# Two ways of cutting the first expert's 448 rows in a fused attention and mixture-of-experts kernel

## The chip, the cores and the metric

The kernel runs on one core of a Trainium2 chip. The metric is the device time of one execution in microseconds (us). The core has a matrix engine (TensorE, PE in the rows; its weight loads are PEld), a vector engine (VectorE, DVE), a scalar engine (ScalarE, ACT), a general engine (GpSimd, POOL) and a queue that issues DMAs (SyncE, SP). Each of them works through its own instructions in the order in which they stand, and waits for the others by semaphores.

## The reference, cut to what matters

Attention over 2 batches of 768 tokens is followed by a mixture of 8 experts, in which each of the 1536 tokens goes to two experts, and by a dense layer pair. `attn_out` below is the attention's output as rows of 512 numbers.

```python
logits = x @ w_gate                                   # x: (1536, 512), the attention's output
noisy_logits = logits + np.log1p(np.exp(x @ w_noise)) * noise
top2 = np.argpartition(-noisy_logits, 2, axis=1)[:, :2]
...
for e in range(8):
    for k in range(2):
        mask = top2[:, k] == e
        h = np.maximum(x[mask] @ w1[e], 0.0)          # 512 -> 1024
        out[mask] += top2_w[mask, k, None] * (h @ w2[e])   # 1024 -> 512
...
h = x @ w_in                                          # the dense pair, 512 -> 2048 -> 512
return (h - np.tanh(h)) @ w_out
```

With the inputs of `setup_inputs()` the experts 0 to 7 get 358, 364, 398, 396, 398, 396, 379 and 383 tokens; of expert 0's, 182 are of batch 0 and 176 of batch 1.

## The kernel before

**Precision.** Every matrix product is made of three products in the type fp32r: a high part of the weights by a high part of the rows, the same weights by the low part of the rows, and the low part of the weights by the high part of the rows. So a tile `hh` holds the high part `hh` and the low part `hl` of a hidden layer, and `xh`, `xl` are the parts of an expert's input rows.

**Segments.** An expert has room for 448 rows (`CAP`). Expert 0 is cut in two segments, the others are one segment each; `segs` (L109) lists them as expert, part, first row, rows, and the number of 128-row blocks next to a shorter tail. Segment 0 is the first 192 rows of expert 0 (`FIRST`), all of which come from batch 0; segment 1 is its other 256 rows. Either has two blocks, of 96 and of 128 rows.

**The products of a segment.** The hidden layer has 1024 units, in eight steps f of 128. In a step the first layer makes 12 products (4 pieces of the depth by 3), whose columns are the segment's rows; `h_out` then lets ScalarE write `hh` (L1306) and VectorE `hl` (L1308). The second layer takes three products of 512 columns for each block (`y_mm`, L1315 to L1317); only the third of them reads `hl`. A short tail of rows is not a block: its high and low parts stand side by side as one stationary operand (`tail_arm`, L1282). The first layer of segments 1 and later chooses among several widths at run time (`ARMS`, `pick_arm`), by the number of rows that an expert got; the number is written by VectorE into `arm` and loaded by TensorE.

**Work in the gaps.** Segment 0 can be computed while batch 1's gate is still being worked out: the gate is a chain of small steps that goes back and forth between VectorE and TensorE. `seg_fine` yields after each piece of segment 0 (half a first layer of a step, or one block's second layer), and `fill` hands pieces out between the steps of the gate: `FILL` and `FILL2` are the numbers of pieces, `left` counts what remains, and `KEEP` pieces are held back for after the gate. `TX` says at which values of `left` segment 1's input rows are transposed (`trans_x`). From the attention to the end of the gate the order on TensorE, VectorE, ScalarE and SyncE is the order in which the code issues; GpSimd's, and the stretch after the gate, follow a scheduler until the order is written by hand again.

**The gate of batch 1.** Its steps, in order: `gate_mm` (L639), the logits and the two best experts on VectorE (L642 to L760, ending in the table `M`), the running counts on TensorE (L776), `where` (L779), six one-hot tables `hot` for the rows that segment 1 takes (`mark`, L819), their products on TensorE (`find`, L828), the indices `xidx` (L829) and two gathers by GpSimd (L835); then the totals (L924, L928), the number of rows for `arm` (L930 to L918), the excess over `CAP` (`exs`, `cmi`), and the target rows `sidx` (L854). With `sidx` GpSimd scatters the tokens to the experts' places in the tensor `Xg`: 12 indirect DMAs of 128 rows each (L858).

**After the gate.** Segment 1's eight steps run. During them SyncE stores segment 0's result (L1343) and loads segment 2's input from `Xg` (L1215, L1218), which needs the scatters; VectorE writes the table `yidx` (L854, a second use of the helper); and TensorE transposes segment 2's rows in steps 5 and 6 of segment 1 (L1228). Then come segments 2 to 8 and the dense pair.

Of the kernel before, what the change touches and what calls it, by code (L numbers as in the profile page):

```python
# [9 lines left out]
F16 = mybir.dt.float16  # L10
# [15 lines left out]
TX = (4, 4, 2, 2)  # L26
# [10 lines left out]
CAP = 448  # L37
# [19 lines left out]
KEEP = 8  # L57
# [4 lines left out]
FIRST = 192  # L62
# [5 lines left out]
ARMS = {0: ((104, 0), (128, 0)),  # L68
# [20 lines left out]
def body(tc, q, k, v, proj, w_gate, w_noise, noise, w1, w2, w_in, w_out, out):  # L89
# [19 lines left out]
    segs = [(0, 0, 0, FIRST, 2), (0, 1, FIRST, CAP - FIRST, 2)]  # L109
# [5 lines left out]
    with ExitStack() as ctx:  # L115
# [489 lines left out]
        idx0 = gx.tile([128, 2], F16, name="idx0")  # L605
        xidx = gx.tile([128, 2], I32, name="xidx")
# [214 lines left out]
        def find(b):  # L821

            ps = bank("a")
            cols = lambda t: [t.rearrange("p (q j) -> p j q", j=2)[:, j] for j in range(2)]
            mms = [(j, id16, idx0[:, j:j + 1]) for j in range(2 * b)]
            mms += [(j, l_, ids[:, b * NC + c:b * NC + c + 1]) for c in range(NC) for j, l_ in enumerate(cols(hot(b, c)))]
            for n, (j, l_, r_) in enumerate(mms):
                nc.tensor.matmul(ps[:, j:j + 1], l_, r_, start=(n == 0), stop=(n >= len(mms) - 2), skip_group_check=True)  # L828
            nc.vector.tensor_copy(xidx if b else idx0, ps[:, 0:2])  # L829

        def gather_x():

            t = hd["xy"][:, 2:4]
            for j in range(2):
                nc.gpsimd.indirect_dma_start(out=t[:, j], out_offset=None, in_=Xd,  # L835
                                             in_offset=bass.IndirectOffsetOnAxis(ap=xidx[:, j:j + 1], axis=0))
            xgs[1] = (t, None)
# [382 lines left out]
        def trans_x(n, dc):  # L1220
# [6 lines left out]
            for j, m_ in enumerate([m] * nb + [128] * (tail > 0)):  # L1227
                nc.tensor.transpose(ps[:, j * m:j * m + m_], xgs[n][0][:m_, j, ck(dc)], ident[:m_, :m_])  # L1228
# [90 lines left out]
        def y_banks(n):  # L1319
            return [bank(t) for t in ("cc" if n == 0 else "dd" if n < B else "ccdd")]  # L1320
# [41 lines left out]
        def seg_fine(n):  # L1362
# [5 lines left out]
            for f in range(NF + 1):  # L1368
                if f < NF:
# [45 lines left out]
        left = [4 * NF]  # L1415
# [388 lines left out]
```

## Time and profile before

| | us |
|---|---|
| runs of the kernel before | 874.85, 876.32, 876.75; median 876.32 |
| the profiled execution | 875.33 |
| its span, first to last instruction | 873.4 |
| TensorE busy | 858.3 (98% of the span) |
| VectorE busy | 665.9 (76%) |
| ScalarE busy | 537.5 (62%) |
| GpSimd busy | 399.7 (46%) |

The span leaves out 1.9 us that lie around it. TensorE is busy nearly all the time, in all of the 40 slices of the page; but that share is no statement on any one stretch. The stretches that the change touches are the gate of batch 1 (272 to 297 us of the span) and segment 1 (301 to 329 us). There the order of the waits is what counts.

### The profile page before, as it was taken

What the parts mean: (1) busy time and instruction counts of PE and PEld (TensorE: products, weight loads), DVE (VectorE), ACT (ScalarE), POOL (GpSimd) and SP (SyncE); (2) the same over time, 40 slices, a digit from 0 to 9 for tenths busy, and PEclk for the clock granted to TensorE, in tenths of its full rate; (3) what the DMA queues carried; (4) which work ended last, traced back from release to release, by engine and by line L of the source; (5) the groups of instructions that cost most, each with busy time, mean ns of one, the idle gap of its engine ahead of it and who ended that gap; (6) DMA issues with size and microseconds to landing.
All of it is one profiled execution on the core that took longest, in us unless ns stands there. A gap on an engine that the chain in (4) does not pass through costs nothing.

```text
span 873.4 us, 13678 instructions
## 1 busy us (share of the span) xinstructions
PE 858.3 (98%) x4621; PEld 673.4 (77%) x4621; DVE 665.9 (76%) x1275; ACT 537.5 (62%) x1028; POOL 399.7 (46%) x390
## 2 busy tenths in 40 slices
PE   8999999999999999999999999999999999999998
PEld 3556555555556889798988889898899999999996
DVE  7688778778775654989798979967886676677665
ACT  7667668667455244545444544567787677677665
POOL 6687787798776644210000008521432622632322
PEclk9999999999999999999999999999999999999999
DMA  5646645411133688797977978563300200200001
GB/s 129 151 116 201 211 127 175 153 43 37 53 112 104 217 288 270 237 323 240 306 259 255 309 262 298 193 238 120 94 22 1 88 22 1 85 25 0 25 13 37
DMA packets 111980, 127.52 MB, mean 146 GB/s; under 512 B 33744, under 2 KB 82944, under 8 KB 111888
## 3 DMA queue, kind: packets, MB, share of 16 engines
q1 hardware_dynamic: 105680, 110.52, 40.0%
q0 software_dynamic: 5008, 15.49, 5.2%
q8 instruction: 57, 0.93, 0.4%
q10 hardware_dynamic: 1200, 0.30, 0.2%
q14 instruction: 35, 0.29, 0.1%
HBM read 82.81 MB, written 41.18 MB: 142 GB/s over the span
## 4 chain that ended last, share of the span: by engine, by line
PE 57%; DVE 4%; ACT 2%; issue 1%; DMA 1%; POOL 0%; SPq 0%; DVEq 0%; ACTq 0%; POOLq 0%
PE bank L1275 13%; PE bank L1317 9%; PE bank L1315 9%; PE bank L1316 9%; PE bank L1237 4%; PE bank L1235 4%; PE bank L1236 4%; PE bank L1282 2%; PE bank L1228 1%; DVE wt L1010 1%; DMA xy<-Xg 1%; DVE g_u L1604 1%; PE bank L1573 1%; DMA wraw<-in_moe_w_dram 0%; DVE hh L1622 0%
## 5 line engine op out<-in xcount | busy, mean ns | idle before, releaser
L1315 PE MATMUL bank<-wt,hh 128*128 128x512 f32 (+1 forms) x392 | 155.5, 397 | 2.2 <-PEq L1253 1.2
L1317 PE MATMUL bank<-wt,hh 128*128 128x512 f32 (+1 forms) x392 | 155.2, 396 | 1.3 <-DVE hh L1308 1.2
L1316 PE MATMUL bank<-wt,hh 128*128 128x512 f32 (+1 forms) x392 | 153.9, 393 | 0.0
L1597 POOL TENSOR_TENSOR g_th<-g_h,g_th 128x384 f32<-128x384 f32 x64 | 66.9, 1046 | 183.3 <-ACT g_th L1596 182.6
L1275 PE MATMUL bank<-xh,wt 128*128 128x400 f32 (+3 forms) x512 | 139.0, 335 | 0.0
L481 ACT ACTIVATE p<-bank 128x384 f32<-128x384 f32 x192 | 91.8, 488 | 67.5 <-PE bank L480 56.7
L446 DVE TENSOR_REDUCE mx<-bank 128x1 f32<-128x384 f32 x192 | 103.3, 551 | 36.6 <-PE bank L445 34.5
L1010 POOL TENSOR_TENSOR wt<-wraw,wt 128x512 fp32r<-128x512 f32 x30 | 48.7, 1642 | 143.5 <-DVE xy L1347 137.1
L1275 PEld LDWEIGHTS bank<-xh,wt 128*128 128x128 f32 x512 | 92.7, 188 | 1.8 <-issue 0.3
L1011 ACT ACTIVATE wt<-wraw 128x1024 fp32r<-128x1024 f32 x75 | 78.9, 1055 | 19.4 <-PE bank L1317 17.0
L1317 PEld LDWEIGHTS bank<-wt,hh 128*128 128x128 f32 (+1 forms) x392 | 73.1, 186 | 20.5 <-DVE hh L1308 2.1
L1237 PE MATMUL bank<-xh,wt 128*128 128x384 f32 x256 | 86.4, 337 | 0.0
L1315 PEld LDWEIGHTS bank<-wt,hh 128*128 128x128 f32 (+1 forms) x392 | 73.2, 187 | 17.0 <-issue 2.4
L1235 PE MATMUL bank<-xh,wt 128*128 128x384 f32 x256 | 86.2, 337 | 0.0
L1236 PE MATMUL bank<-xl,wt 128*128 128x384 f32 x256 | 86.0, 336 | 0.0
L1275 PE MATMUL bank<-xl,wt 128*128 128x400 f32 (+3 forms) x256 | 84.7, 331 | 0.9 <-DVE xl L1230 0.9
L514 POOL TENSOR_TENSOR ps<-ps,p 128x768 f32<-128x768 f32 x45 | 82.3, 1829 | 7.3 <-ACT p L481 3.1
L1306 ACT ACTIVATE hh<-bank 128x448 fp32r<-128x448 f32 (+2 forms) x72 | 36.1, 502 | 79.5 <-issue 22.7
L1316 PEld LDWEIGHTS bank<-wt,hh 128*128 128x128 f32 (+1 forms) x392 | 73.2, 187 | 13.2
L505 PE MATMUL bank<-p,v 128*64 128x384 f32 x384 | 83.1, 512 | 0.0
L479 PE MATMUL bank<-qc,kb 108*128 108x384 f32 (+1 forms) x192 | 78.9, 411 | 1.1 <-DVE qc L469 1.0
L1010 DVE TENSOR_TENSOR wt<-wraw,wt 128x1024 fp32r<-128x1024 f32 (+1 forms) x64 | 73.9, 1158 | 3.9 <-ACT wt L1011 3.6
(319 smaller groups left out, 1819.7 us busy)
## 6 DMA issues: line engine op xcount, KB each, us to landing
wraw<-in_moe_w_dram SPq DMA_DIRECT2D x118, 256.0 KB
cv_t<-in_moe_w_in_dram SPq DMA_DIRECT2D x16, 512.0 KB
cv_t<-in_moe_w_out_dram SPq DMA_DIRECT2D x16, 512.0 KB
W2f<-cv_w SPq DMA_DIRECT2D x16, 512.0 KB
wraw<-W2f SPq DMA_DIRECT2D x16, 512.0 KB
Xg<-zero SPq DMA_DIRECT2D x14, 512.0 KB
xy<-Xg SPq DMA_DIRECT2D x7, 768.0 KB
Y<-xy SPq DMA_DIRECT2D x7, 768.0 KB
```

The source lines that it names most:

```text
L446: nc.vector.tensor_reduce(MX[i % 2][:, c, hf:hf + 1], ps[:, :HF], op=ALU.max, axis=AX.X)
L481: nc.scalar.activation(hd["p", i, kc][:, half(hf)], ps[:, :HF], AF.Exp, scale=float(D) ** -0.5)
L505: nc.tensor.matmul(hd["o", i][hf * D:(hf + 1) * D, :HF], raw["v", g][:, par, kc], hd["p", i, kc][:, half(hf)], start=(kc == 0), stop=(kc = ...
L514: eng.tensor_tensor(t, hd["p", i, 0] if kc == 1 else t, hd["p", i, kc], op=ALU.add)
L1010: low = lambda eng, h: eng.tensor_tensor(t[:, 1, h], r[:, h], t[:, 0, h].bitcast(F32), op=ALU.subtract)
L1235: nc.tensor.matmul(ps[:, :n], ws(0, dc), xh[:, dc, :n], start=(dc == 0), stop=False)
L1236: nc.tensor.matmul(ps[:, :n], ws(0, dc), xl[:, dc, :n], start=False, stop=False)
L1237: nc.tensor.matmul(ps[:, :n], ws(1, dc), xh[:, dc, :n], start=False, stop=(dc == KD4 - 1))
L1275: nc.tensor.matmul(col(ps), t[:, w_, 0, ck(dc)], col(x_[l_][:, dc]), start=(dc == 0 and (w_, l_) == (0, 0)), stop=(dc == KD4 - 1 and w_ == 1))
L1315: nc.tensor.matmul(ps[:m], a, t[:, 0, 1], start=first, stop=False)
L1316: nc.tensor.matmul(ps[:m], a, t[:, 1, 1], start=False, stop=False)
L1317: nc.tensor.matmul(ps[:m], l, t[:, 0, 1], start=False, stop=last)
```

## The change

Expert 0 is cut at row 128 instead of 192. Segment 0 becomes one block of 128 rows; segment 1 becomes 320 rows, in two blocks of 128 and a tail of up to 64. That is three blocks for expert 0 instead of four.

- Segment 0's first layer hands its 128 columns to each product twice (`twice`), so a product has 256 columns.
- Segment 1 gets four widths instead of two. A row count of at most 360 takes the first: two times 116 columns, no tail. Choosing takes two more VectorE instructions (L917) for `arm`.
- `find` and `gather_x` handle 320 rows: the one-hot tables have 320 columns instead of 256, there are three products for each token chunk instead of two (18 and 21 instead of 12 and 14), one more copy after each (L829), and three gathers instead of two. `trans_x` of segment 1 makes three transposes for each piece instead of two, and that of segment 0 one instead of two.
- There are 24 pieces of segment 0 instead of 32. `FILL` and `FILL2` stay; `KEEP` and `TX` become 4 and (1, 1, 0, 0).
- The accumulators in PSUM: segment 0 takes one bank, segment 1 three (`y_banks`).

```diff
-TX = (4, 4, 2, 2)
+TX = (1, 1, 0, 0)
...
-KEEP = 8
+KEEP = 4
...
-FIRST = 192
+FIRST = 128
...
-ARMS = {0: ((104, 0), (128, 0)),
+ARMS = {0: ((116, 0), (128, 0), (128, 16), (128, 64)),
...
-    segs = [(0, 0, 0, FIRST, 2), (0, 1, FIRST, CAP - FIRST, 2)]
+    segs = [(0, 0, 0, FIRST, 1), (0, 1, FIRST, CAP - FIRST, 2)]
...
-            cols = lambda t: [t.rearrange("p (q j) -> p j q", j=2)[:, j] for j in range(2)]
-            mms = [(j, id16, idx0[:, j:j + 1]) for j in range(2 * b)]
+            cols = lambda t: [t[:, 0:256].rearrange("p (q j) -> p j q", j=2)[:, j] for j in range(2)] + [t[:, 256:NL]]
+            some = lambda j: slice(0, 128 if j < 2 else NL - 256)
+            mms = [(j, id16[some(j), some(j)], idx0[some(j), j:j + 1]) for j in range(3 * b)]
...
-            nc.vector.tensor_copy(xidx if b else idx0, ps[:, 0:2])
+            o_ = xidx if b else idx0
+            nc.vector.tensor_copy(o_[:, 0:2], ps[:, 0:2])
+            nc.vector.tensor_copy(o_[some(2), 2:3], ps[some(2), 2:3])
...
-            t = hd["xy"][:, 2:4]
-            for j in range(2):
-                nc.gpsimd.indirect_dma_start(out=t[:, j], out_offset=None, in_=Xd,
-                                             in_offset=bass.IndirectOffsetOnAxis(ap=xidx[:, j:j + 1], axis=0))
+            t = hd["xy"][:, 1:4]
+            for j in range(3):
+                r = slice(0, 128 if j < 2 else NL - 256)
+                nc.gpsimd.indirect_dma_start(out=t[r, j], out_offset=None, in_=Xd,
+                                             in_offset=bass.IndirectOffsetOnAxis(ap=xidx[r, j:j + 1], axis=0))
...
-            return [bank(t) for t in ("cc" if n == 0 else "dd" if n < B else "ccdd")]
+            return [bank(t) for t in ("c" if n == 0 else "cdd" if n < B else "ccdd")]
...
+                    twice = lambda a_: a_[:, None, :rows].to_broadcast([128, 2, rows])
...
-                            nc.tensor.matmul(ps[:, :rows], ws(t, w_, dc), x_[:, dc, :rows], start=st_, stop=sp_)
+                            nc.tensor.matmul(ps[:, :2 * rows].rearrange("p (t n) -> p t n", t=2), ws(t, w_, dc), twice(x_[:, dc]),
+                                             start=st_, stop=sp_)
...
-        left = [4 * NF]
+        left = [3 * NF]
```

The order on two engines moves with it, since a step of segment 0 is three pieces instead of four while `FILL` stays. In the rows below a buffer's number tells tiles apart; the weights of steps 2, 3, 4 and 6 are wt_1522, wt_1908, wt_2286 and, in the changed kernel, wt_3432.

TensorE, before, at the running counts of the gate (L776): the second layer of step 2 stands ahead of them, and step 3's first layer ahead of that.

```order
L1376 MATMUL bank2_3275<-xh_3296,wt_1908 128x192
L1315 MATMUL bank4_3497<-wt_1143,hh_3493 96x512
...
L1315 MATMUL bank5_3496<-wt_1522,hh_3591 96x512
L1316 MATMUL bank5_3496<-wt_1522,hh_3591 96x512
L1317 MATMUL bank5_3496<-wt_1522,hh_3591 96x512
L1315 MATMUL bank4_3497<-wt_1522,hh_3591 96x512
L1316 MATMUL bank4_3497<-wt_1522,hh_3591 96x512
L1317 MATMUL bank4_3497<-wt_1522,hh_3591 96x512
L776 LDWEIGHTS before_182
L776 MATMUL bank1_3662<-M_198,before_182 128x48
```

The same place now.

```order
L1321 MATMUL bank5_3492<-wt_1522,hh_3583 128x512
L1381 MATMUL bank3_3277<-xh_3296,wt_2286 128x256
...
L1319 MATMUL bank5_3492<-wt_1908,hh_3649 128x512
L1320 MATMUL bank5_3492<-wt_1908,hh_3649 128x512
L1321 MATMUL bank5_3492<-wt_1908,hh_3649 128x512
L776 LDWEIGHTS before_182
L776 MATMUL bank1_3673<-M_198,before_182 128x48
```

Step 4's first layer and step 3's second layer have moved ahead of the running counts.

VectorE, before, from the totals to the excess.

```order
L928 COPY tots<-bank_3724 128x24
L930 TENSOR_TENSOR cnt<-tots 1x8
L931 TENSOR_TENSOR cnt<-cnt,basev 1x1
L915 TENSOR_SCALAR acc<-cnt 1x1
L918 CAST arm<-acc 1x1
L935 TENSOR_TENSOR exs<-tots 128x8
L936 TENSOR_TENSOR exs<-exs,capv 128x8
L937 TENSOR_SCALAR exs<-exs 128x8
L1308 SCALAR_TENSOR_TENSOR hh<-bank_3275,hh 128x192
L940 TENSOR_REDUCE cmx<-exs 128x1
```

The same place now.

```order
L932 COPY tots<-bank_3747 128x24
L1312 SCALAR_TENSOR_TENSOR hh<-bank_3277,hh 128x128
L934 TENSOR_TENSOR cnt<-tots 1x8
L935 TENSOR_TENSOR cnt<-cnt,basev 1x1
L919 TENSOR_SCALAR acc<-cnt 1x1
L921 SCALAR_TENSOR_TENSOR acc<-cnt,acc 1x1 x2
L922 CAST arm<-acc 1x1
L939 TENSOR_TENSOR exs<-tots 128x8
L940 TENSOR_TENSOR exs<-exs,capv 128x8
L941 TENSOR_SCALAR exs<-exs 128x8
L944 TENSOR_REDUCE cmx<-exs 128x1
```

The low part of a step of segment 0 stood between L937 and L940, that of step 5; now a low part, that of step 6, stands right behind the totals, and ahead of everything that is worked out from them.

TensorE, now, around that step's first layer and the totals (L928, L931).

```order
L1321 MATMUL bank5_3492<-wt_2286,hh_3667 128x512
L1381 MATMUL bank3_3277<-xh_3296,wt_3432 128x256
...
L928 LDWEIGHTS onesb_180
L928 MATMUL bank1_3747<-M_198,onesb_180 128x8
...
L931 MATMUL bank1_3747<-M_198,onesb_180 128x8
L1381 MATMUL bank3_3277<-xh_3296,wt_3432 128x256
```

Step 6's first layer is cut in two by the totals; before, two second layers of step 3 stood ahead of the totals and the first layer of step 5 behind them.

## Rows read from the trace of the kernel before

**Rows 1.** Stretches: us; busy PE, PEld, DVE, ACT, POOL; granted clock; DMA share, GB/s.
```profile
272.00:297.00 25.00, 24.66 (x216) 20.48 (x214) 18.03 (x84) 7.12 (x15) 14.48 (x14) 1.00 0.37 124
297.00:320.00 23.00, 21.79 (x142) 18.69 (x141) 13.45 (x41) 10.11 (x19) 13.94 (x13) 1.00 0.85 298
```

**Rows 2.** TensorE in order of time, segment 1: start, us, instructions, [idle before <-releaser].
```profile
316.20 0.50 PE L1317 MATMUL bank<-wt,hh 128*128 128x512 f32 x1 [0.91 <-DVE hh L1308]
...
320.14 0.49 PE L1228 MATMUL bank<-ident,xy 128*128 128x128 f32 x3
320.82 0.76 PE L1228 MATMUL bank<-ident,xy 128*128 128x128 f32 x5 [0.18 <-DMA xy<-Xg]
```

**Rows 3.** VectorE in order of time, segment 1.
```profile
314.15 0.17 DVE L854 CAST yidx<-g_p 128x12 int32<-128x12 f32 x1 [2.43 <-DMA Xg<-x,sidx]
...
314.60 1.22 DVE L1010 TENSOR_TENSOR wt<-wraw,wt 128x1024 fp32r<-128x1024 f32 x1
315.73 0.42 DVE L1308 SCALAR_TENSOR_TENSOR hh<-bank,hh 128x256 fp32r<-128x256 f32 x1
```

**Rows 4.** SyncE's queue in order of time: the store of segment 0, the load of segment 2.
```profile
314.04 0.33 SPq L1343 DMA_DIRECT2D Y<-xl  x1
...
314.92 0.69 SPq L1218 DMA_DIRECT2D xy<-Xg  x1
```

**Rows 5.** GpSimd in order of time: a gather, the first scatter after the gate, the last.
```profile
290.23 0.96 POOL L835 DMA_INDIRECT xy<-Xd,xidx  x1 [0.30 <-issue]
294.54 1.78 POOL L858 DMA_INDIRECT Xg<-x,sidx  x1 [3.35 <-DVE sidx L854]
...
309.42 0.98 POOL L858 DMA_INDIRECT Xg<-x,sidx  x1 [0.31 <-issue]
```

**Rows 6.** VectorE in order of time, the gate of batch 1.
```profile
285.86 0.35 DVE L1308 SCALAR_TENSOR_TENSOR hh<-bank,hh 128x192 fp32r<-128x192 f32 x1
286.64 0.22 DVE L779 SCALAR_TENSOR_TENSOR where<-bank,late,M 128x6 f32<-128x6 f32 x1 [0.43 <-PE bank L776]
286.90 1.29 DVE L819 TENSOR_SCALAR xT<-zero,where 128x256 f16<-128x256 f16 x6
...
290.33 0.18 DVE L928 COPY tots<-bank 128x24 f32<-128x24 f32 x1 [1.19 <-PE bank L927]
290.55 0.16 DVE L930 TENSOR_TENSOR cnt<-tots 1x8 f32<-1x8 f32 x1
...
292.12 0.36 DVE L1308 SCALAR_TENSOR_TENSOR hh<-bank,hh 128x192 fp32r<-128x192 f32 x1 [0.40 <-ACT hh L1306]
292.39 0.15 DVE L940 TENSOR_REDUCE cmx<-exs 128x1 f32<-128x8 f32 x1
...
294.09 0.17 DVE L854 CAST sidx<-g_p 128x12 int32<-128x12 f32 x1
294.19 2.36 DVE L1010 TENSOR_TENSOR wt<-wraw,wt 128x1024 fp32r<-128x1024 f32 x2
```

**Rows 7.** TensorE in order of time, gate of batch 1, then the start of segment 1.
```profile
286.13 0.20 PE L776 MATMUL bank<-M,before 128*128 128x48 bf16 x1
...
288.31 0.45 PE L1315 MATMUL bank<-wt,hh 128*96 128x512 f32 x1
...
289.76 0.45 PE L924 MATMUL bank<-M,onesb 128*128 128x8 bf16 x12
...
290.15 0.34 PE L1376 MATMUL bank<-xh,wt 128*128 128x192 f32 x1
...
291.56 0.39 PE L1315 MATMUL bank<-wt,hh 128*96 128x512 f32 x1
...
301.09 0.26 PE L1275 MATMUL bank<-xh,wt 128*128 128x208 f32 x1
```

**Rows 8.** The chain that ended last: start, us, what; twelve products of 208, then of 372 columns.
```profile
305.32 1.32 PE bank L1275 x12
...
325.18 2.05 PE bank L1275 x12
```

More of the change, by code (lines that the diff above doesn't have):

```diff
@@ L604, in body @@
         ids = zero[:, NL // 2 + 64:NL // 2 + 64 + B * NC // 2].bitcast(F16)
-        idx0 = gx.tile([128, 2], F16, name="idx0")
-        xidx = gx.tile([128, 2], I32, name="xidx")
+        idx0 = gx.tile([128, 3], F16, name="idx0")
+        xidx = gx.tile([128, 3], I32, name="xidx")
         where = gx.tile([128, B, NC], F32, name="where")
@@ L823, in find @@
             ps = bank("a")
-            cols = lambda t: [t.rearrange("p (q j) -> p j q", j=2)[:, j] for j in range(2)]
-            mms = [(j, id16, idx0[:, j:j + 1]) for j in range(2 * b)]
+            cols = lambda t: [t[:, 0:256].rearrange("p (q j) -> p j q", j=2)[:, j] for j in range(2)] + [t[:, 256:NL]]
+            some = lambda j: slice(0, 128 if j < 2 else NL - 256)
+            mms = [(j, id16[some(j), some(j)], idx0[some(j), j:j + 1]) for j in range(3 * b)]
             mms += [(j, l_, ids[:, b * NC + c:b * NC + c + 1]) for c in range(NC) for j, l_ in enumerate(cols(hot(b, c)))]
             for n, (j, l_, r_) in enumerate(mms):
-                nc.tensor.matmul(ps[:, j:j + 1], l_, r_, start=(n == 0), stop=(n >= len(mms) - 2), skip_group_check=True)
-            nc.vector.tensor_copy(xidx if b else idx0, ps[:, 0:2])
+                nc.tensor.matmul(ps[some(j), j:j + 1], l_, r_, start=(n == 0), stop=(n >= len(mms) - 3), skip_group_check=True)
+            o_ = xidx if b else idx0
+            nc.vector.tensor_copy(o_[:, 0:2], ps[:, 0:2])
+            nc.vector.tensor_copy(o_[some(2), 2:3], ps[some(2), 2:3])
         def gather_x():
-            t = hd["xy"][:, 2:4]
-            for j in range(2):
-                nc.gpsimd.indirect_dma_start(out=t[:, j], out_offset=None, in_=Xd,
-                                             in_offset=bass.IndirectOffsetOnAxis(ap=xidx[:, j:j + 1], axis=0))
+            t = hd["xy"][:, 1:4]
[3 more added lines that the diff above has]
+                                             in_offset=bass.IndirectOffsetOnAxis(ap=xidx[r, j:j + 1], axis=0))
             xgs[1] = (t, None)
@@ L1226, in trans_x @@
             ps = bank("a")
-            for j, m_ in enumerate([m] * nb + [128] * (tail > 0)):
+            for j, m_ in enumerate([m] * nb + [tail if n < B else 128] * (tail > 0)):
                 nc.tensor.transpose(ps[:, j * m:j * m + m_], xgs[n][0][:m_, j, ck(dc)], ident[:m_, :m_])
```

## The prediction

> **What bounds the kernel now.** I read first the stretches [rows 1]: in the gate of batch 1 TensorE works 24.66 of 25 us, so a product taken out there looks like time won. Then I read who ends TensorE's waits behind that stretch, in order of time. In segment 1 TensorE waits twice: 0.91 us at 316.20 for the low part of a step, and 0.18 us at 320.82, in the middle of the transposes of segment 2's rows, for the load of these rows [rows 2]. Both waits hang on one thing that TensorE has no part in. On VectorE the low part (315.73) stands behind a weight split (314.60), and that behind the table `yidx`, for which VectorE sat idle 2.43 us until the last scatter had landed, at 314.15 [rows 3]. On SyncE's queue segment 0's store went out at 314.04, at the same landing, and the load of segment 2's rows behind it, its last part at 314.92 [rows 4]; in the rows it lands just before 320.82. So a second chain runs beside TensorE's products: gate, `sidx`, 12 scatters, landing, low part and load, transposes. TensorE arrives 0.9 us early at the one place and 0.2 us early at the other. The time is set by that chain as far as the transposes, and by TensorE's products behind them. Products saved ahead of 316 us lengthen the wait there; they shorten nothing unless the scatters land earlier too. The question is what the change does to `sidx`.
>
> **What it takes from TensorE.** The second layer of expert 0 loses 24 products of 512 columns. Six of them took 1.45 us (288.31 to 289.76) [rows 7], 0.24 each with their start: 5.6 us. Segment 0's 96 first-layer products grow from 192 to 256 columns. The trace has no such product of 256; twelve of 192 took 1.41 us (290.15 to 291.56) [rows 7], twelve of 208 took 1.32 and twelve of 372 took 2.05 us [rows 8]. So 192 and 208 cost alike, about 0.11 each, and 372 costs 0.171. For 256 I take 0.118, near the narrow rows since it is nearer to them; the ends are 0.11 and, on a line from 208 to 372, 0.128. That adds 0.8 us (0 to 1.7). Segment 1's 96 products go from 208 to 232 columns: 0.3 us by the same reckoning (0 to 0.9). Thirteen more of the tiny products of `find`, at 0.45 us for twelve [rows 7], add at most 0.5 us; the tail's one product 0.24. The transposes go from eight to four for segment 0 and from eight to twelve for segment 1: nil. TensorE is left with some 3.8 us less to do before the transposes of segment 2.
>
> By the Trainium skill ("TensorE: Matmul & The Clock Gate", section "Back-to-back issue gap") an isolated product takes its columns at 2.4 GHz and 2.5 ns, which makes 82 ns for 192 columns and 109 for 256, and would price the doubled columns at 2.6 us instead of 0.8. The rows disagree at 192 columns (0.11), so I keep theirs.
>
> **What it does to `sidx`, step by step.** The trace shows all the pieces; only their order is new.
>
> (1) The running counts (L776) began at 286.13 [rows 7]. Step 3's second layer now stands ahead of them, and its third product needs the low part of step 3, which VectorE writes only behind the table `M`: 285.86, 0.35 long [rows 6]. It is ready near 286.2, the product takes 0.23, the counts begin near 286.5: **+0.4 us** (0.3 to 0.5), and `where` (286.64) with them.
>
> (2) The six one-hot tables behind `where` took 1.29 us at 256 columns [rows 6]. At 320 they cost at least nothing more and at most a quarter more, 0.32; I take **+0.2**, because small instructions of VectorE in the same rows last 0.15 whatever they hold. The last products of `find` wait for the last table, so TensorE goes on at about 288.9 instead of 288.31.
>
> (3) From there to the totals TensorE had six second-layer products, 1.45 us [rows 7]. Now it has three (0.7) and half a first layer (0.7): the same.
>
> (4) The totals come 0.6 later, VectorE's copy (290.33) [rows 6] near 290.9. Directly behind it VectorE now has the low part of step 6, whose second half of the first layer TensorE begins behind the totals: 0.7 us, and the lag to the low part, 0.56 (291.56, end of step 5's products, to 292.12) [rows 6, 7]. VectorE waits until about 292.0, and `cnt` begins near 292.2 instead of 290.55 [rows 6]: **+1.65**. What is queued behind that wait is everything that leads to `sidx`.
>
> (5) From `cnt` to `sidx` the rows have 3.54 us (290.55 to 294.09) [rows 6]. The low part of step 5, which stood in between, cost 0.40 of waiting and 0.27 of its own: about **-0.65**. Two more small instructions for `arm`, at about 0.2 each (290.33 to 290.55) [rows 6]: **+0.4**. So `sidx` comes near 295.5: **+1.4 us** in all. Without growth of the tables it is +1.2, with a quarter and slow products +1.75.
>
> **From `sidx` to the end.** GpSimd sat idle 3.35 us ahead of the first scatter [rows 5]. The second gather began at 290.23 and takes 1.26 with its gap [rows 5]; 0.6 later and with a third behind it, GpSimd is free near 293.4, and the third is covered; were `sidx` two microseconds earlier it would not be. The twelve scatters go out between 294.54 and 309.42 [rows 5], one behind the other, whatever TensorE does, so they land 1.4 later, near 315.5. VectorE's low part follows at the distance that it had (314.15 to 315.73 [rows 3]), and TensorE's third product of that step at 317.6 instead of 316.20. TensorE waits for it for some 3.4 us: it came at 315.3 before (316.20 less 0.91) and comes near 314.2. (Not 3.8 earlier, since it is held up already on the way: behind `sidx` VectorE has two weight splits, 2.36 us [rows 6], so until 298.0; then the low part of step 7, 0.3, which the last product of segment 0 waits for; then come six transposes, some 0.7 (five took 0.76 to their last end [rows 2]). Segment 1 begins near 299.2 instead of 301.09 [rows 7], and spends about 0.8 more: on the low parts of rows just transposed, for which no product is left as cover, on the tail's product and on wider columns.) From the third product to the transposes lie 3.94 us (316.20 to 320.14) [rows 2]: 321.5, and the point where TensorE waited for the load comes at 322.0. The load lands 1.4 later, less what segment 0's store no longer carries: 128 KB at about 0.3 MB/us [rows 1], 0.4 us; so near 321.8, no wait there. TensorE goes on at 322.0 instead of 320.82: **+1.2 us**. Behind it the work is as before, but for segment 1's tail bank, whose two evacuations segment 2's tail waits for: 0.1. The sum is **+1.3 us**.
>
> The profiled execution took 875.33, the median of three is 876.32, their mean 875.97. 875.33 + 1.3 is 876.6; against the median it is 877.6. I predict 877.1, between the two.
>
> **The rivals.**
>
> *The saving gets through.* If VectorE's wait for the landing is an ordering that falls away, or the low part of step 6 is no obstacle because TensorE reaches it sooner, `sidx` stays where it was or comes earlier, and part of the 3.8 us arrives: 871.5 if all, 873.5 if half. For it speaks TensorE's share of 24.66 in 25 us [rows 1]; against it that the idle 2.43 us on VectorE and the store at 314.04 end at one landing [rows 3, 4], and that in the new order of VectorE the wait is written down. Chance 0.16.
>
> *The clock falls.* The granted clock is 1.00 in both stretches [rows 1], that is 2.4 GHz, and the longest wait in them is 0.91 us [rows 2]. A wait of 3.4 us is new. If TensorE's clock dropped to 1.2 GHz behind it, each microsecond of products would take two: up to 3.9 us more by the transposes, so 879 to 881. It decides from the point where the wait at 316.20 is long enough. No row at the lower level stands against or for it. Chance 0.12.
>
> The Trainium skill ("TensorE: Matmul & The Clock Gate", Part 1) says that an idle TensorE falls back to the lower level and has to earn the higher one again; no row here shows a fall.
>
> *A wider arm.* Expert 0 has 358 rows by the reference and 360 is the first arm's limit. If the kernel counted over 360, tail products would come back, two a step at 0.24: 3.4 us, of which the wait of 3.4 us swallows those ahead of 316 and 1.4 remain: 878.5. Chance 0.02.
>
> **How the numbers follow.** The forecast, a chain that comes 1.3 us later (0.9 to 2.0), has 0.70; with the spread of the runs shown (874.85 to 876.75) it lies within 875.5 and 878.6. I split it 0.48 within 0.2% of before (1.75 us, about what a measurement of this kernel can tell from no change) and 0.22 slower. Faster: 0.16, the first rival. Slower: 0.22, 0.12 and 0.02, so 0.36. The range goes from 873.8, half of the saving, to 879.2, the lower part of the clock's fall.
>
> **What would show it.** In the changed trace: `cnt` behind a wait of about 1 us for the low part of step 6; `sidx` near 295.5; the last scatter 1.4 us later; one TensorE wait of 3 to 4 us in segment 1 for a low part, behind the idle time before `yidx`; first-layer products of segment 0 at 0.11 to 0.13 each. I am wrong if `sidx` is not later, if that wait is short, or if the granted clock falls behind it.

## The result, and the profile after

The changed kernel takes 883.66 us (median of seven runs, 879.69 to 885.36), the kernel before 875.01 (seven runs, 874.7 to 876.82): a ratio of 1.0083, with a 95% interval of 1.0058 to 1.0108. The prediction was 877.1, in a range up to 879.2. The profiled execution of the changed kernel took 885.01, that of before 875.33, so the two traces differ by 9.7 us.

First the stretches of the changed kernel's TensorE, with columns: stretch in us, its length, TensorE busy (instructions), granted clock, DMA share, GB/s. The counterpart is [rows 1], where the clock is 1.00 throughout.

```profile
272.00:297.00 25.00, 22.65 (x199) 1.00 0.39 127
297.00:320.00 23.00, 19.81 (x90) 0.63 0.73 252
295.00:300.00 5.00, 0.97 (x4) 0.70 0.20 64
300.00:305.00 5.00, 3.83 (x15) 0.50 0.91 297
305.00:310.00 5.00, 5.00 (x17) 0.50 1.04 364
310.00:315.00 5.00, 5.00 (x25) 0.60 0.96 374
315.00:320.00 5.00, 5.00 (x36) 1.00 0.44 122
```

Between 295 and 300 TensorE works one microsecond in five, and for the ten behind it runs at 0.50, that is at 1.2 instead of 2.4 GHz. Its instructions in order of time (start, us, instruction, idle time before and what ended it) show why:

```profile
294.46 0.28 PE L1381 MATMUL bank<-xl,wt 128*128 128x256 f32 x1
299.03 0.80 PE L1381 MATMUL bank<-xh,wt 128*128 128x256 f32 x2 [4.29 <-DVE wt L1014]
299.62 0.42 PE L1381 MATMUL bank<-xl,wt 128*128 128x256 f32 x1
...
303.98 1.87 PE L1232 MATMUL bank<-ident,xy 128*128 128x128 f32 x6 [1.17 <-DVEq L1489]
...
308.99 0.56 PE L1279 MATMUL bank<-xh,wt 128*128 128x232 f32 x1
309.35 0.42 PE L1279 MATMUL bank<-xl,wt 128*128 128x232 f32 x1
...
315.87 0.28 PE L1279 MATMUL bank<-xl,wt 128*128 128x232 f32 x1
...
329.38 1.04 PE L1232 MATMUL bank<-ident,xy 128*128 128x128 f32 x8
```

The third product of step 7 of segment 0 multiplies with the low part of that step's weights, and waits 4.29 us for it. Behind the wait everything takes twice its time until 314.04: products of 232 columns start 0.21 us apart (309.35 to 309.56) and later 0.12 (315.87 to 315.99). Segment 2's transposes begin at 329.38 without a wait of their own; before, at 320.14 [rows 2]. On VectorE, in order of time:

```profile
291.06 0.16 DVE L831 CAST xidx<-bank 128x2 int32<-128x2 f32 x1 [1.60 <-PE bank L829]
...
293.04 0.18 DVE L932 COPY tots<-bank 128x24 f32<-128x24 f32 x1 [1.33 <-PE bank L931]
294.17 0.29 DVE L1312 SCALAR_TENSOR_TENSOR hh<-bank,hh 128x128 fp32r<-128x128 f32 x1 [0.94 <-ACT hh L1310]
294.38 0.14 DVE L934 TENSOR_TENSOR cnt<-tots 1x8 f32<-1x8 f32 x1
...
297.64 0.17 DVE L858 CAST sidx<-g_p 128x12 int32<-128x12 f32 x1
297.75 2.36 DVE L1014 TENSOR_TENSOR wt<-wraw,wt 128x1024 fp32r<-128x1024 f32 x2
```

The two weight splits at L1014 stand right behind `sidx`, as they did before [rows 6]; the first of them is the low part that TensorE waits for. `sidx` comes at 297.64 instead of 294.09, 3.55 us later, and the split with it. Why `sidx` is so late is seen on TensorE, in the counts, `find` and the totals:

```profile
287.33 0.20 PE L776 MATMUL bank<-M,before 128*128 128x48 bf16 x1
...
289.42 1.61 PE L829 MATMUL bank<-zero,xT 128*128 128x1 f16 x18
...
292.47 0.46 PE L928 MATMUL bank<-M,onesb 128*128 128x8 bf16 x12
```

The 18 tiny products of `find` take 1.61 us; the changed kernel's first `find`, near 282 us, takes 1.61 too. The 12 products of the kernel before took 0.45 in its first `find` and 0.54 in its second:

```profile
282.35 0.45 PE L828 MATMUL bank<-zero,xy 128*128 128x1 f16 x12
...
287.92 0.54 PE L828 MATMUL bank<-zero,xT 128*128 128x1 f16 x12
```

On GpSimd the scatters follow `sidx` as they did:

```profile
298.09 1.77 POOL L862 DMA_INDIRECT Xg<-x,sidx  x1 [3.12 <-DVE sidx L858]
...
312.97 0.97 POOL L862 DMA_INDIRECT Xg<-x,sidx  x1 [0.30 <-issue]
```

**An account of the 9.7 us.** The wait costs 4.29; the wait at the branch, 1.17 where the kernel before had 0.30, costs 0.87; of the 15.0 us at half clock (299.03 to 314.04) 1.17 are that wait, and the other 13.8 do the work of 6.9 and cost 6.9. Against that stand the prediction's saving in products, 4.3 without those of `find`, and the two waits of segment 1 that are gone, 0.91 and 0.18 [rows 2]. `find` costs 1.16 more the first time and 1.07 the second. 4.29 + 0.87 + 6.9 - 4.3 - 1.1 + 2.2 is 8.9. Some 0.8 of the 9.7 us stay open; most of it comes behind the transposes of segment 2, which begin 9.2 us later than before.

The runs themselves tell clock from wait. The seven runs of the changed kernel have mean granted clocks, over the whole execution, of 0.997 (879.69 and 880.27 us), 0.994 (880.89), 0.992 (883.66) and 0.990 (885.01, 885.26, 885.36). The quickest are 4.7 us above the kernel before. A mean clock of 0.997 over 878 us is a loss of up to 2.6 us, and the account without its clock term is 2.0; together about the 4.7. What the rest have on top goes with the clock.

### The profile page after: what moved, and what is told of

Read it like the earlier page. It is cut to its first block, busy times and chain, and to the rows that moved or that the text cites. A ratio compares the mean times of both kernels' runs of the same rounds, so it can differ in the third digit from the quotient of the medians.

```text
span 883.2 us, 13686 instructions
## 1 busy us (share of the span) xinstructions
PE 864.0 (98%) x4611; PEld 678.6 (77%) x4611; DVE 667.9 (76%) x1288; ACT 537.6 (61%) x1028; POOL 403.5 (46%) x391
## 4 chain that ended last, share of the span: by engine, by line
PE 54%; DVE 4%; ACT 2%; issue 1%; POOL 0%; DVEq 0%; POOLq 0%
PE bank L1279 12%; PE bank L1321 9%; PE bank L1319 8%; PE bank L1320 8%; PE bank L1241 4%; PE bank L1239 4%; PE bank L1240 4%; PE bank L1286 2%; PE bank L1232 1%; DVE wt L1014 1%; DVE g_u L1610 1%; PE bank L1579 1%; DVE g_u L1622 0%; ACT hh L1623 0%; DVE hh L1628 0%
## 5 line engine op out<-in xcount | busy, mean ns | idle before, releaser
L1319 PE MATMUL bank<-wt,hh 128*128 128x512 f32 x384 | 152.9, 398 | 2.4 <-PEq L1257 1.2
L1321 PE MATMUL bank<-wt,hh 128*128 128x512 f32 x384 | 152.5, 397 | 0.2
L1320 PE MATMUL bank<-wt,hh 128*128 128x512 f32 x384 | 151.3, 394 | 0.0
L1279 PE MATMUL bank<-xh,wt 128*128 128x400 f32 (+3 forms) x512 | 141.5, 340 | 0.0
L1014 POOL TENSOR_TENSOR wt<-wraw,wt 128x512 fp32r<-128x512 f32 x30 | 48.7, 1641 | 139.5 <-DVE xy L1351 133.4
L1279 PEld LDWEIGHTS bank<-xh,wt 128*128 128x128 f32 x512 | 94.7, 193 | 1.5
L1321 PEld LDWEIGHTS bank<-wt,hh 128*128 128x128 f32 x384 | 72.4, 188 | 18.3 <-DVE hh L1628 1.8
L1319 PEld LDWEIGHTS bank<-wt,hh 128*128 128x128 f32 x384 | 72.5, 189 | 17.4 <-issue 2.9
L1320 PEld LDWEIGHTS bank<-wt,hh 128*128 128x128 f32 x384 | 72.6, 189 | 12.6
L1014 DVE TENSOR_TENSOR wt<-wraw,wt 128x1024 fp32r<-128x1024 f32 (+1 forms) x64 | 74.4, 1166 | 4.1 <-ACT wt L1015 3.7
```

Source lines behind the costliest of these rows:

```text
L1014: low = lambda eng, h: eng.tensor_tensor(t[:, 1, h], r[:, h], t[:, 0, h].bitcast(F32), op=ALU.subtract)
L1279: nc.tensor.matmul(col(ps), t[:, w_, 0, ck(dc)], col(x_[l_][:, dc]), start=(dc == 0 and (w_, l_) == (0, 0)), stop=(dc == KD4 - 1 and w_ == 1))
L1319: nc.tensor.matmul(ps[:m], a, t[:, 0, 1], start=first, stop=False)
L1320: nc.tensor.matmul(ps[:m], a, t[:, 1, 1], start=False, stop=False)
L1321: nc.tensor.matmul(ps[:m], l, t[:, 0, 1], start=False, stop=last)
```

## The experiments

**The chips.** The chips that ran the experiments take 887 us for the kernel before, not 875. A profile of it there (e5) shows pauses that the first chip did not have, one near 286.5 us on VectorE and on TensorE, which waits for it, one near 311 us on TensorE, VectorE and ScalarE; here TensorE behind the first pause, in order of time:

```profile
288.14 0.20 PE L776 MATMUL bank<-M,before 128*128 128x48 bf16 x1 [2.10 <-DVE M L760]
```

The stretches of TensorE behind it (busy, granted clock, DMA):

```profile
290.00:295.00 5.00, 4.72 (x38) 0.50 0.18 55
295.00:300.00 5.00, 5.00 (x20) 0.50 0.19 52
```

TensorE at the second pause:

```profile
310.69 0.27 PE L1275 MATMUL bank<-xh,wt 128*128 128x208 f32 x1
316.30 0.80 PE L1315 MATMUL bank<-wt,hh 128*128 128x512 f32 x1 [5.33 <-issue]
```

ScalarE there:

```profile
315.86 0.38 ACT L1306 ACTIVATE hh<-bank 128x256 fp32r<-128x256 f32 x1 [6.54 <-remote]
```

No row names a cause: ScalarE had the products it needed from 310.96 on. So absolute times don't carry over from the first chip, and a clock in 286 to 320 has to be read together with these pauses. Nor are the pauses alike from trace to trace: TensorE's later one lasts 5.33 us here, 1.50 in e1, 4.15 in e6 and 6.09 in e14. Ratios are to the kernel before, run beside it on the same chip; the changed kernel has 1.0077 and 1.0060 there against 1.0083 on the first.

| run | what is different | us | ratio (95%) |
|---|---|---|---|
| e6, e14 | the changed kernel | 894.78, 892.75 | 1.0077 (1.0059 to 1.0095), 1.0060 (1.0038 to 1.0082) |
| e1 | step 7's low part earlier | 888.65 | 1.0012 (0.9998 to 1.0025) |
| e2, e7 | e1, `find` all 128 wide | 887.73, 888.07 | 1.0000 (0.9979 to 1.0021), 1.0005 (0.9994 to 1.0016) |
| e3 | dummy products in the wait | 889.39 | 1.0020 (1.0007 to 1.0033) |
| e4, e13 | kernel before, with a wait of 3.23, 4.39 us | 889.32, 890.26 | 1.0030 (1.0010 to 1.0050), 1.0044 (1.0027 to 1.0061) |
| e8, e15 | e7, the changed kernel, columns streamed once | 891.16, 893.88 | 1.0034 (1.0021 to 1.0047), 1.0087 (1.0071 to 1.0104) |
| e9, e16 | e7, three more edits ahead of the branch | 887.08, 886.86 | 0.9997 (0.9978 to 1.0016), 1.0003 (0.9985 to 1.0021) |
| e10 | those edits in the kernel before | 888.86 | 1.0017 (1.0003 to 1.0030) |
| e11 | e1, `find` ordered by width | 887.38 | 1.0003 (0.9988 to 1.0019) |
| e12 | `find` all 128 wide, alone | 891.27 | 1.0040 (1.0017 to 1.0063) |

### e1: the low part of step 7 earlier

```diff
 def find(b):
     ...
+    if b:
+        hd["lows"].pop(0)()
     o_ = xidx if b else idx0
```

> The changed kernel, with one instruction moved: VectorE splits the low part of step 7's weights while it waits for the second find (1.60 us at 291.06 in the changed kernel, the split takes 1.18) instead of behind sidx. Theory 1 (TensorE's 4.29 us wait for that low part, and the fall of the granted clock behind it, are the loss): the wait is gone, the granted clock stays at 1.00 over 297 to 320, and of the 9.7 us at least 7.5 come back. Theory 2 (with the wait gone, the later sidx binds: it stands 3.55 us later than before, and segment 1's transposes of the loaded rows with it): TensorE waits 3 us or more in segment 1 for the low part behind yidx or for the loaded rows, and the time is 878 to 879. Rival (cutting the part or streaming it twice costs the time by itself): the time stays at 882 or above, with no wait at step 7.

1.0012 where the changed kernel has 1.0077 on the same chip: 5.8 of 6.8 us come back, and the 4.8 us wait for `wt` is gone. So theory 1 holds for the wait. The rival, that cut or doubled columns are the loss, falls: e1 has both. Theory 1's clock did not come: it is 0.86 in 300 to 305 and 0.50 in 305 to 310, behind two shorter waits (2.12 us in step 7 and 1.99 at the branch). And part of what came back may be the chip's: of the 6.4 us between the two traced runs (894.86 in e6, 888.46) the later pause, 1.50 instead of 4.15, makes 2.7. Theory 2's wait in segment 1 for the loaded rows isn't seen, but there the chip's pauses give the rows time. A smaller wait took the place of the old one, in the same step:

```profile
301.42 0.49 PE L1383 MATMUL bank<-xh,wt 128*128 128x256 f32 x2 [2.12 <-DVE acc L921]
```

`acc` is nothing that a product needs. The instructions on `arm` in the same stretch show what stands there (count, shortest, median and longest ns, first and last start):

```profile
L924 DVE CAST arm<-acc x2: 142/150/158, 300.3 to 301.8; 1x1 int32<-1x1 f32 x1, 1x7 int32<-1x7 f32 x1
L1249 PEldq TENSOR_LOAD <-arm x1: 494/494/494, 300.5 to 300.5; - x1
```

TensorE reads expert 0's `arm` into a register here (300.5), and can't until VectorE has written it (300.3).

### e2 and e7: every product of find 128 wide

```diff
-cols = lambda t: [...] + [t[:, 256:NL]]
+cols = lambda t: [...] + [t[:, NL - 128:NL]]
```

(with e1's edit, and the copies, the gather and the transposes to match)

> The kernel of e1_low_early, and the third product of each chunk in find is 128 columns wide (the last 128 of the 320, of which 64 repeat) instead of 64; the gather then fetches 128 rows for it, 64 of them unused. Theory 3 (products with 64 and with 128 output rows in turn are slow, 18 in 1.61 us; 18 alike take 12's 0.45 times 1.5, some 0.7 us): each find takes 0.7 to 0.8 us, sidx stands 1.8 to 2.2 us earlier than in e1_low_early, and the time falls by as much if theory 2 holds (876 to 877), or not at all if it doesn't. Rival (the find's length comes from the count of products, not their widths): 1.6 us again, and the time of e1_low_early.

Eighteen products took 0.62 us where they took 1.61:

```profile
294.19 0.62 PE L828 MATMUL bank<-zero,xT 128*128 128x1 f16 x18
```

Theory 3 holds for `find`. The ratio is 1.0000 and the median 0.9 us less than e1's, with intervals that overlap, so a gain in time is not shown; `sidx`, which was to come 1.8 to 2.2 us earlier, came 0.74 earlier (302.53 against 303.27), in a run that paused 3.69 us near 287 where e1 paused 1.93. e7 is the same kernel:

> As e2: low part of step 7's weights split in the wait for the second find, all products of find 128 wide. On a chip without the pause, theory 1 and 2: no wait at step 7, the clock at 1.00 over 290 to 315, sidx 1.5 us later than before, 875.5 to 877.5. If cutting or doubling costs by itself: 880 or above.

1.0005. The chip had the pauses again, so the case for which 875.5 to 877.5 was given did not come up. The clock was not at 1.00 in 290 to 315 as expected: 0.50 in 290 to 295, behind the chip's pause, and 0.50 in 305 to 310.

### e3: dummy products in the wait

```diff
 for w_, x_, st_, sp_ in (...):
+    if (f, dc, w_) == (NF - 1, 0, 1):
+        warm(18)
```

> The changed kernel, with 18 dummy products of 512 columns (some 0.23 us each, 4.1 us) set on TensorE just ahead of the product that waits 4.29 us for step 7's low part; nothing else moves. It parts the wait from the clock. If the clock falls because TensorE stood idle: it stays at 1.00 over 299 to 314, the stretch runs 7.5 us faster, and the time is 877.5 to 879 although the 4.3 us are lost as before. Rival (the clock falls for another reason, such as the doubled columns): it is 0.50 from 299 to 314 again, and the time is 883 to 886.

The clock stays up behind the place of the wait (stretches of TensorE):

```profile
300.00:305.00 5.00, 4.00 (x21) 1.00 0.10 35
305.00:310.00 5.00, 3.93 (x22) 1.00 1.00 296
310.00:315.00 5.00, 3.54 (x27) 1.00 1.06 377
```

and the ratio is 1.0020, 3.5 to 5 us less than the changed kernel's, although the product starts no sooner (304.11, where the changed kernel in e6 has 303.73). In e6 the same stretches have 0.83, 0.83 and 0.51. The mean clocks of all runs agree: 0.992 to 0.998 in e3, 0.987 to 0.990 in e6, 0.983 to 0.994 in e14. So an idle TensorE is what lets the clock fall here, and the fall is more than half of the loss. By the Trainium skill ("TensorE: Matmul & The Clock Gate", Part 1) an idle TensorE drops to the lower level; this pair agrees.

### e4 and e13: the same wait in the kernel before

```diff
-for fn_ in hd.pop("lows"):
+for fn_ in 4 * hd["lows"][:1] + hd.pop("lows"):    # e13: 5
```

> The kernel before, where VectorE does the split of step 7's low part five times instead of once (four times 1.18 us, 4.7 more), so that TensorE waits there about as long as it does in the changed kernel; no part of the change is in it. If wait and clock are the whole loss: a wait of about 4.4 us at step 7, the granted clock at 0.50 for some 15 us behind it, and 883 to 887 in all. Rival (the fall needs something of the change): the clock stays at 1.00 and the time is 877 to 879.5, the wait less what the two branch waits and the rows' chain give back.

The wait came out at 3.23 us, shorter than meant, and the ratio at 1.0030, 2.7 us. That is the rival's size (2 to 4.5 us above 875), but not its clock, which didn't stay at 1.00 (0.75 in 305 to 310). So e13 made the wait as long as the changed kernel's:

> The kernel before with the split of step 7's low part done six times (five times 1.18 us more than the kernel needs; e4 had four and a wait of 3.23 us). The wait at step 7 should be 4.4 us, about what the changed kernel has (4.29 and 4.77). If such a wait costs its length and a fall of the clock in either cut: a ratio of 1.006 to 1.009, as e6. If it costs its length alone, as e4 did (1.0030): 1.004 to 1.0045. If the fall belongs to the wait only where doubled products follow: 1.004 too, with the granted clock at 1.00 in the 5 us behind the wait.

TensorE in order of time, the end of the wait in e13:

```profile
307.82 0.74 PE L1376 MATMUL bank<-xh,wt 128*128 128x192 f32 x2 [4.39 <-DVE wt L1010]
```

1.0044, 3.9 us: the wait's length, no more. Yet the clock did fall behind it (0.76 in 305 to 310, 0.56 in 310 to 315). But the kernel before has a half-clock stretch of its own there, behind its pause at 311 (e5), and in e13 the later pause is 1.70 us instead of 5.33, with the clock at 1.00 behind it. So on these chips the added wait and its fall of the clock seem to stand in for a pause and a fall that came anyway; that is an argument, not shown. What is shown: on these chips such a wait costs the old cut about its length. Whether the changed kernel's wait costs more there is not: beside e13 it has 1.0060 (e14), and the intervals overlap. On the first chip, without pauses, the changed kernel lost 8.65 us with a wait of 4.29; the old cut with an added wait was not run there.

### e5, e6 and e14: both kernels again

> The kernel before, unchanged, looked at on the chip of this call. The chip of e1 to e4 ran it at 887.73 us (875.01 on the first chip), and all four kernels there show a pause of 1.9 to 3.7 us on TensorE, VectorE and ScalarE near 286.5 us that the kernel before didn't have on the first chip, with the granted clock at 0.50 behind it. If the pause belongs to the chip: here either 874 to 877 without it, or 886 to 890 with it and with a fall of the clock in 286 to 300. Rival (the four edits caused it): the kernel before shows no pause wherever it is slow.

The pause belongs to the chip, not to the edits (the rows ahead of the table).

> The changed kernel, unchanged, beside the kernel before on the same chip. On a chip where the kernel before runs at 875: 880 to 885, with the 4.29 us wait for step 7's low part and the clock at 0.50 behind it. On one where the kernel before itself pauses near 286.5 and loses the clock: within 0.3 per cent of it, since a clock that is down already can't be lost again.

Here the expectation was wrong: 1.0077, as on the first chip, with a wait of 4.77 us. A clock that falls on its own doesn't make the change free. In e14:

> The changed kernel once more, beside e13 on one chip: 1.006 to 1.010, a wait of 4.3 to 4.8 us for step 7's low part and the clock at 0.50 for most of the 10 us behind it. In runs whose mean clock is 0.995 or more the time should be 4 us or so nearer to the kernel before than in those at 0.990 or less, since the fall is then short.

The median is 1.0060, with a wait of 4.71. Three of its ten runs have a mean clock of 0.994 and 887.58 to 888.57 us, the other seven 0.983 to 0.992 and 892.67 to 894.92: two outcomes of one kernel, 4 to 7 us apart, about as expected. The clock at 0.50 for most of 10 us is not in the profiled run, where it is 0.80 and 1.00 in the two stretches behind the wait; a pause of 6.09 us follows there.

### e8 and e15: the columns streamed once

```diff
-nc.tensor.matmul(ps[:, :2 * rows]..., ws(t, w_, dc), twice(x_[:, dc]), ...)
+nc.tensor.matmul(ps[:, :rows], ws(t, w_, dc), x_[:, dc, :rows], ...)
```

> As e7, with the first part's first-layer products streamed once (128 columns, from rows 8 some 0.9 to 1.0 us for 12 products against 1.42 for 256 columns): eight steps, 3.4 us less of TensorE's work in them, some of it beside transposes and waits. If TensorE's work ahead of the branch were the bound, 3 us faster than e7; if the chain of sidx, scatters and loaded rows binds (theory 2), the same as e7 within 0.7 us, or slower where TensorE then waits or its clock falls.

1.0034 beside 1.0005 for e7: 2.6 us slower, with intervals apart. There is hardly less work, either: ahead of the pause products of 128 columns start 0.11 us apart (e15, 281.08 to 281.42 for three), as those of 192 and 208 columns do. The 0.9 to 1.0 us for twelve that the expectation took are 1.3.

> The changed kernel with the first part's first-layer products streamed once (128 columns). TensorE arrives at step 7 some 2 to 3 us sooner, and the low part comes no sooner: the wait grows to 6 to 8 us, and the time is that of the changed kernel within 2 us (1.006 to 1.010). If doubling is what costs, the time falls by 3 us or more (1.004 or less); if doubled products hold the clock, it rises by as much.

1.0087 beside 1.0060 for e14: 2.4 us slower by the medians, but the intervals overlap. The wait is shorter (3.53 us), not longer. What is clearly lower is the mean clock: 0.977 to 0.983 against 0.983 to 0.994 in e14, and 0.979 to 0.987 in e8 against 0.983 to 0.994 in e7. The stretches of TensorE show where. e15:

```profile
290.00:295.00 5.00, 5.00 (x34) 0.50 0.01 2
295.00:300.00 5.00, 5.00 (x34) 0.50 0.40 131
```

and the changed kernel in e14:

```profile
290.00:295.00 5.00, 5.00 (x47) 0.66 0.01 2
295.00:300.00 5.00, 3.66 (x35) 1.00 0.36 116
```

Behind the same pause the products of 256 columns get the full clock back, those of 128 don't until after the branch; in 295 to 300 the clock is 0.90 in e7 and 0.50 in e8. The two traced runs of e14 and e15 took alike all the same (892.75 and 892.93 us), since e15 had less of waits and pauses for what it lost by the clock (a later pause of 2.78 us against 6.09). So doubling costs nothing here and, in e7 against e8, pays 2.6 us, by the clock as far as the traces tell. On the first chip, which has no fall ahead of the wait, that isn't tried.

### e9 and e16: three more edits ahead of the branch; e10: the same in the old cut

e9 is e7 with:

```diff
 def totals():
     ...
+    hd["lows"].pop(0)()
     nc.vector.tensor_copy(tots, ...)
 def excess():
     ...
-    pick_arms(1, 1, E)
...
-load_arm(1)
...
+nc.vector.scalar_tensor_tensor(arm2, XL[1][0:1, 0, 0:1]..., 0.0, arm[:, 0:1], op0=ALU.mult, op1=ALU.add)
 fill(left[0])
+AV[1] = nc.tensor.value_load(arm2[0:1, 0:1], ...)
 ...
 both_step(1, 0)
+pick_arms(1, 1, E)
```

(`arm2` takes a zero from the first transposed rows, which binds the load of the register to a place behind the branch.)

> The kernel of e7 with three more edits of what stands ahead of the branch: VectorE splits the second deferred low part (expert 1's step 0) in its wait for the totals (1.93 us in e2) instead of behind sidx; the arms of experts 1 to 7 are worked out behind the branch (0.7 us of VectorE's chain before sidx); and TensorE reads the first expert's arm into its register behind the transposes, not in the middle of step 7's first layer, where e1, e2 and e7 waited 1.5 to 2.1 us for it (the row says released by acc, the order of instructions shows the register load there). Theory 4 (what is left of the loss in e7 are these waits, each made by VectorE's chain being late): no wait inside step 7, the wait at the branch 1 us or less instead of 2, sidx 0.7 us earlier than in e7, and a ratio to the kernel before of 0.995 to 0.998. Rival (the cut's own work is a loss, or the pauses of this chip absorb any gain): 1.000 again or more.

> The kernel of e9 once more, on the chip of e13 to e15. If this chip runs the kernel before at 875 without the pauses: 0.996 to 1.000 by theory 4, with no wait inside step 7. If at 887 with the pauses: 0.999 to 1.001 as e9.

No wait is left inside step 7, as expected, and the time is 0.9997 and 1.0003: no gain, where theory 4 had 0.995 to 0.998. It is the number of theory 4's rival, and the one that e16 gives for a chip with pauses. The wait went on to the branch. TensorE's next instructions in e16, and GpSimd's third gather:

```profile
297.39 0.39 PE L1321 MATMUL bank<-wt,hh 128*128 128x512 f32 x1
300.71 0.41 PE L1232 MATMUL bank<-ident,xy 128*128 128x128 f32 x2 [2.94 <-DVEq L1490]
302.83 1.28 PE L1232 MATMUL bank<-ident,xy 64*128 64x64 f32 x4 [1.71 <-DMA xy<-Xd,xidx]
```

```profile
295.93 0.95 POOL L838 DMA_INDIRECT xy<-Xd,xidx  x1 [0.31 <-issue]
```

TensorE is done with what stands ahead of the branch at 297.8. VectorE gets to the branch only behind `sidx` (299.37), and the rows of the third gather, one that the old cut doesn't have, land 1.71 us after the first transposes. 4.65 us of waiting in all, where the kernel before waits 0.30.

> The kernel before (192 and 256 rows, four blocks) with the same edits as e9 apart from find, whose products are alike there already. If these edits pay by themselves, whatever the cut: the same ratio as e9. If they only mend what the cut makes late (theory 4): nothing stood in these places before, so 0.998 to 1.002, and the difference to e9 is what cutting in three blocks is worth with its waits out of the way, 0 to 3 us.

1.0017: the same edits mend nothing in the old cut, they cost it a little. Between e9 and e10 lie 0.2%, 1.8 us, and their intervals overlap; so that is about what the new cut is worth, if anything, once the waits are out that could be moved.

### e11: find in another order; e12: find alone

```diff
+mms.sort(key=lambda m_: m_[0])
 for n, (j, l_, r_) in enumerate(mms):
```

(with e1's edit, and `stop` on the last product of each column)

> The kernel of e1 with find's products in another order: all even columns first, then all odd ones, then the 64-wide ones together, instead of the three in turn for each chunk of 128 rows. Theory 3a (going from 128 output rows to 64 and back is what costs): find takes 0.6 to 0.8 us as in e2. Rival 3b (a 64-wide product is slow by itself): 1.2 to 1.6 us as in e1. The time follows e2 or e1, which differ by 0.1 per cent, so only find's length and sidx tell.

```profile
291.46 0.50 PE L830 MATMUL bank<-zero,xT 128*128 128x1 f16 x6
...
291.85 0.29 PE L830 MATMUL bank<-zero,xT 128*128 128x1 f16 x6
...
292.18 0.35 PE L830 MATMUL bank<-zero,xT 128*64 128x1 f16 x6
```

The six 64-wide products (`128*64` in the row) take 0.35 us together, no more than six wide ones; the first `find` takes 0.73 in all. Products of one width that go through the three columns in turn are quick too (e2, 0.62). So it is the turn from one width to the other that costs: eleven turns among 18 products, 1.0 us (1.61 less 0.62). By the Trainium skill ("TensorEngine Tiling (Array Packing)", "Key Properties") a change of tiling mode drains TensorE; that page lists 128x64 as a configuration of its own ("Available Configurations"), and these rows agree.

e12 is the edit of e2 without that of e1.

> The changed kernel with find's third product 128 wide and nothing else: the low part of step 7 stays behind sidx. Find is shorter by 0.6 to 1.0 us, sidx and the low part stand 1.0 to 2.0 us earlier, TensorE's wait for the low part is 3 to 4 us instead of 4.77 (e6). If the loss goes by the length of the wait alone, 1 to 2 us come back of the 7 (ratio 1.0055 to 1.0065); if the fall of the clock behind any such wait is most of it, about the same; if the wait becomes short enough that the clock holds, 1.002 or less.

1.0040 with a wait of 4.82 us: the low part comes earlier, but so does TensorE, and the wait is not shorter as expected. So the wait's length doesn't hang on `find`. In two of nine runs the clock holds better (0.996, 886.41 and 886.42 us); in the others it is 0.985 to 0.990, and 889.45 to 893.73.

## Why the prediction was wrong, step by step

**What held.** The bound was read rightly as far as `sidx`: VectorE's wait for step 6's low part ahead of `cnt`, written down from the order alone, is there (0.94 us, 294.17). Step (4) put 1.05 us more between the totals and `cnt`; it is 1.12 (1.34, where it was 0.22 [rows 6]). Step (5) gave -0.25 and it is -0.28 (3.26 for 3.54 us [rows 6]). The tables (step (2), +0.2) took 0.07 more, within the predicted bounds. Products of 256 columns start 0.118 us apart, as taken (twelve in 1.42 us, 285.19 to 286.61). (The 24 products saved, at 0.24, are 5.8 us and not the 5.6 of the sum; that moves nothing.) The third gather is covered on GpSimd, and the scatters, the store and the load moved with `sidx`.

**The mis-sized term.** Steps (1) to (3) price `find` at the same 0.45 us for twelve products, "at most 0.5" more for thirteen. It takes 1.16 more the first time and 1.07 the second, because its products go back and forth between two widths (e11 and e2). The first one delays the counts (287.33, +1.2 instead of +0.4), both together the totals (+2.7 instead of about +0.6). `sidx` comes 3.55 us later, not 1.4; these 2.1 us are, by the sum of the two, `find`. The row that [rows 7] has for 0.45 us is that of the totals' twelve products (L924); the `find` of before took about as long, but it has one width, and I took its price for a bound.

**The step that failed.** The prediction names the two weight splits behind `sidx` and counts them as work that VectorE has to get through ("so until 298.0") before step 7's low part of the hidden units. It does not ask whose weights they are. The first split is the low part of step 7's weights, and TensorE needs it at the third product of step 7, not at the last product of the segment. In the trace of before TensorE reached that point at 295.84:

```profile
295.73 0.27 PE L1376 MATMUL bank<-xl,wt 128*128 128x192 f32 x1
295.84 0.39 PE L1376 MATMUL bank<-xh,wt 128*128 128x192 f32 x2
```

The split was done near 295.4, 1.2 us behind its start at 294.19 [rows 6]. That is a slack of under half a microsecond, so no wait stood in that trace. Everything that put `sidx` later put this product later by as much, and TensorE, with less to do, came sooner. The wait was there by the prediction's own numbers: with `sidx` at 295.5 the split is done near 296.8, and TensorE, with totals at 290.4 and the 2.27 us that it takes from there (292.47 to 294.74), arrives near 292.6, so it waits some 4 us. `find` put both later alike, which is why the wait is 4.82 us in e12 with `find` short. So the failed step is this wait, which the prediction put at nothing without a reason: it measured 4.29 us, and the half clock behind it cost 6.9 more. `find` comes on top with 2.2. e1 moves that one instruction and has 5.8 of the 6.8 us back on the experiments' chip, a part of it perhaps by a shorter pause.

**The rival that came true elsewhere.** "The clock falls" had a chance of 0.12, behind a wait in segment 1, with 879 to 881. It fell behind another wait, which ended at 299.03 and not at the predicted 317.6, and lasted 15 us. Three of the seven runs (879.69 to 880.89) lie in the rival's 879 to 881; by another wait and another sum, that is chance. e3 shows that it is the idle time: TensorE kept busy in the wait keeps its clock. The size was low because I let the fall last only until the next point where the chain binds.

**What stays open.** The mechanism of the forecast itself, that the load of segment 2's rows would bind at +1.2 us, is in no run: with the wait, TensorE is some 9 us late there and nothing waits; without it, TensorE paused on the experiments' chips just ahead of that place (1.50 us in e1, 1.77 in e2), longer than the forecast's 1.3. Whether the version without the waits would beat the kernel before on a chip without pauses can't be told from these runs. On the chips that there were, none of the versions beats it.

## What to carry to other kernels

When a chain comes later, list everything queued behind it on its engine, and for each piece who waits for it first, with the slack of that consumer; an instruction that has never shown up as a releaser can have a slack of nothing. When work leaves the busiest engine, ask what it runs into: here weights, then a register load, then the branch, then the gathered rows, each of which had been covered by the work that was removed. A wait of some 4 us on TensorE can cost two to three times its length by the clock (4.29 and 6.9 us on the first chip), so price it at both levels; it need not (3.9 us in all for the 4.39 of e13).

## What the hardware showed that was not expected

Tiny products that alternate between 128 and 64 output rows cost 0.09 us each, against 0.035 (0.62 for 18) when all are alike. One kernel has outcomes 3 to 7 us apart that go with its mean clock (e14, e12, and the seven runs of the changed kernel). Streaming columns twice can be quicker than once (e7 against e8), with TensorE back at its full clock sooner; at that clock products of 128 to 208 columns cost the same 0.11 us. And the same program ran 1.4% longer on other chips, 887 instead of 875 us, with pauses in which an engine had its inputs and did nothing (VectorE near 287 us, ScalarE near 311), whose cause stays open.
